# Convolution band in one skewed DRAM write, and w_in in two equal halves around the x load

## Chip, cores and metric

The kernel runs on one core of one Trainium2 chip. The metric is the device time of one execution, in microseconds (us). Before the change the median of 10 runs is 736.57 us (736.01 to 738.22).

## What is computed

A light convolution over the sequence is followed by a two-layer network with an ELU. The input x is (8, 4096, 192), so there are 32768 tokens of 192 channels; weight is (8, 7).

```python
w = softmax(weight, axis=-1)                  # 8 heads, 7 taps
x_pad = 6 zero rows ahead of each sequence
attn[b, s, h*24+g] = sum_k w[h, k] * x_pad[b, s+k, h*24+g]
h = attn.reshape(32768, 192) @ w_in           # (192, 2048)
g = where(h > 0, h, exp(min(h, 0)) - 1)
out = g @ w_out                               # (2048, 192), float32
```

## The kernel before

**Tiling.** The tokens are cut into 32 super-blocks (index s) of 1024, each in two groups of 512. The hidden width 2048 is cut into 16 slices (index q) of 128. One step n is one slice of one super-block, n = 16 s + q. Each step has two units, one per group of tokens. A unit goes through the engines in this order: three w_in matmuls on PE (L794) into a PSUM bank, exp on ACT (L604) into a ring E of 8 buffers, a clamp on GpSimd (POOL, L555), and on DVE the ELU's join (L675), which writes gT and frees the bank. Later the w_out matmuls on PE (L817) read gT, and ACT evacuates their sums (L608) to be stored by SP (L419).

**Convolution.** From the second super-block on, the convolution is a matmul too (L769). Its stationary operand is Tm, [128 x 8 x 112] bf16: for each head a banded matrix in which the seven softmax taps stand on a diagonal. Its moving operand is xg, rows of x in overlapping windows. ACT evacuates it to csb (L600), and a transposing transfer on SP makes att of it (L462). Each super-block has four such steps (m = 4 s + u).

**The first super-block** goes another way, as Tm isn't there yet: x is loaded to xs by ACT's queue (L567), cast by ACT (L583), transposed on PE (L719, L731) and convolved on PE with seven diagonal matrices `taps` (L747), built on DVE (L645).

**How Tm is made.** DVE works out the softmax, in small steps L620 to L631, and their product with the reciprocal goes to wprb, [128 x 8 x 7] bf16 (L654), in reversed tap order; it is the eighth increment of the semaphore s_set. SP then makes the band through DRAM with three transfers. L841 fills conv_band, [128 x 8 x 134], with zeros from the tile zw, once xs has landed. L851 writes the seven taps of each head into row p at an offset that grows by one element per row. L853 reads columns 6 to 117 of each head back into Tm. Each waits for the one ahead of it to land (s_band, 16 each), and L851 also for s_set at 8.

**Orders.** Each engine works through its own list in order. PE's list comes out of a planner (`emit`, `h_items`, `c_items`, `o_items`) with assumed durations; it is fixed at build time. In it the first convolution matmul (m = 4, in step n = 6) waits for s_band at 48 (L759); it also waits for its xg windows (L761). The first w_in matmul of a step waits for that part of w_in which holds its slice q (L785 to L788). The w_out matmuls wait for their half of w_out (L814).

**GpSimd's queue** issues all loads that cast from fp32. At the start it issues, one after the other, w_in's columns 0 to 511 (`load_w_in(0, ...)`, six transfers), columns 512 to 2047 (six more), the first half of w_out (L512), xg for super-block 1 (two transfers, L483), the second half of w_out, and xg for super-block 2. The clamps follow it in its list.

```python
WCOLS = ((0, 4 * FC), (4 * FC, 16 * FC))
load_w_in(0, 0)
load_w_in(0, 1)
load_w_in(1, 0)
load_w_in(1, 1)
load_w_out(0)
for gr in range(2):
    load_x(1, gr)
load_w_out(1)
for gr in range(2):
    load_x(2, gr)
```

Of the kernel before, what the change touches and what calls it, by code (L numbers as in the profile page):

```python
# [8 lines left out]
BF16 = mybir.dt.bfloat16  # L9
# [3 lines left out]
P = 128  # L13
HP = 64
FC = 128
D = 192
HEADS = 8
KSIZE = 7
CPH = 24
CW = 112  # L20
GS = 512
SUP = 2 * GS
PAD = KSIZE - 1
KW = CW + PAD
TW = P + PAD
# [11 lines left out]
QB = 2  # L37
WARM = (15, 1)
FILL = 1
WCOLS = ((0, 4 * FC), (4 * FC, 16 * FC))  # L40
HALO = 8
XI = SUP // P
MM_H, MM_O, MM_C = 216.0, 82.5, 102.5
AHEAD = 100.0
# [11 lines left out]
def bass_lightweight_conv__then__act_elu_kernel(  # L56
# [220 lines left out]
    def tt_count(n, r):  # L277
        return unit_at[n, r] + 1

    band = nc.dram_tensor("conv_band", (P, HEADS, TW), BF16).ap()  # L280

    with ExitStack() as stack:
        def sbuf(name, shape, dt):
            return stack.enter_context(nc.sbuf_tensor(name, shape, dt))
# [4 lines left out]
        def sema(name):  # L289
            return stack.enter_context(nc.semaphore(name))  # L290

        xg = sbuf("xg", [P, NXB, 2 * NWIN, D], BF16)
        Tm = sbuf("Tm", [P, HEADS, CW], BF16)
# [23 lines left out]
        wex = sbuf("wex", [P, HEADS, KSIZE], FP32)  # L317
        wsum = sbuf("wsum", [P, HEADS], FP32)
        wrs = sbuf("wrs", [P, HEADS], FP32)
        wprb = sbuf("wprb", [P, HEADS, KSIZE], BF16)  # L320
        wch = sbuf("wch", [P, KSIZE], FP32)
        zw = sbuf("zw", [P, TW * HEADS], BF16)
        scr = sbuf("scr", [P, 2], FP32)
# [4 lines left out]
        s_set = sema("s_set")  # L328
# [4 lines left out]
        s_xs = sema("s_xs")  # L333
        s_xh = sema("s_xh")
        s_own = sema("s_own")
        s_xz = sema("s_xz")
        s_cast = sema("s_cast")
        s_tap = sema("s_tap")
# [5 lines left out]
        s_zw = sema("s_zw")  # L344
# [7 lines left out]
        s_band = sema("s_band")  # L352
# [114 lines left out]
        @block.gpsimd  # L467
        def _gpsimd(g: bass.BassGpSimd):
            W = Waits(g)

            def load_x(s, gr):
                b = s % NXB
                if s >= NXB:
                    W(s_cv, CU * (s - NXB))
                if s == NXB:
                    W(s_zw, 1)
                def windows(w0, w1, rows):
                    src = bass.AP(
                        tensor=x_flat.tensor,
                        offset=(s * SUP + gr * GS + w0 * CW - PAD) * D,  # L480
                        ap=[[D, rows], [CW * D, w1 - w0], [1, D]],
                    )
                    g.dma_start(  # L483
                        xg[0:rows, b, 2 * w0 + gr : 2 * w1 : 2, :], src
                    ).then_inc(s_x[b][gr], 16)

                if s == NS - 1 and gr == 1:
                    windows(0, NWIN - 1, P)
                    windows(NWIN - 1, NWIN, GS - CW * (NWIN - 1) + PAD)
                else:  # L490
                    windows(0, NWIN, P)

            def batch_zeros(s):

                W(s_x[s % NXB][0], x_need[s, 0])
                g.memset(xg[0:PAD, s % NXB, 0, :], 0.0).then_inc(s_z)

            def load_w_in(k, half):
                c0, c1 = WCOLS[k]
                for j in range(3):  # L500
                    g.dma_start(  # L501
                        w_in[HP * half : HP * (half + 1), j, c0:c1],
                        bass.AP(
                            tensor=moe_w_in.tensor,
                            offset=8 * j * FF + c0,
                            ap=[[CPH * FF, HEADS], [FF, 8], [1, c1 - c0]],
                        ),
                    ).then_inc(s_w[k], 16)

            def load_w_out(k):  # L510
                q = slice(NQ // 2 * k, NQ // 2 * (k + 1))
                g.dma_start(  # L512
                    w_out[:, q, :], moe_w_out.rearrange("(q p) d -> p q d", p=FC)[:, q, :]
                ).then_inc(s_w[2 + k], 16)

            g.memset(ones[:], 1.0).then_inc(s_id)
            W(s_id, 1)
            g.affine_select(
                out=ident[:],
                in_=ones[:],  # L520
                pattern=[[-1, P]],
                compare_op=ALU.is_equal,
                fill=0.0,
                base=0,
                channel_multiplier=1,
            ).then_inc(s_id)
            for step in range(2):
                W(s_id, 2 + step)
                g.affine_select(
                    out=band16[:],  # L530
                    in_=band16[:] if step else ones[:, 0 : 2 * HEADS],
                    pattern=[[8 * (2 * step - 1), 2 * HEADS]],
                    compare_op=ALU.is_ge,
                    fill=0.0,
                    base=7 * step,
                    channel_multiplier=1 - 2 * step,
                ).then_inc(s_id)
            load_w_in(0, 0)
            load_w_in(0, 1)
            load_w_in(1, 0)  # L540
            load_w_in(1, 1)
            load_w_out(0)
            for gr in range(2):
                load_x(1, gr)
            load_w_out(1)
            for gr in range(2):
                load_x(2, gr)
            for i, (n, u) in enumerate(units):
                s, at_n = divmod(i // 2, NQ)
                if i % 2 == 0 and at_n == ZERO_AT and (s + 2) % SPB == 0 and s + 2 < NS:  # L550
                    batch_zeros(s + 2)
                for to_load in x_before.get(i, ()):
                    load_x(*to_load)
                W(s_exp, i + 1)
                g.tensor_scalar(  # L555
                    out=E[:, i % NE, :],
                    in0=E[:, i % NE, :],
                    scalar1=1.0,
                    scalar2=0.0,
                    op0=ALU.min,  # L560
                    op1=ALU.max,
                ).then_inc(s_clp)
# [50 lines left out]
        def _vector(v):  # L613
            W = Waits(v)
            v.memset(zw[:], 0.0).then_inc(s_zw)  # L615
            v.memset(xbh[:, :, 0, :], 0.0).then_inc(s_xz)
            W(s_id, 4)
            v.tensor_tensor(own[:], band16[:, 0:HEADS], band16[:, HEADS : 2 * HEADS], ALU.add).then_inc(s_own)
            W(s_wq, 16)
# [31 lines left out]
            for at, j in enumerate((3, 0)):  # L651
                W(s_xt, at + 1)
                v.tensor_copy(*transposed(j)).then_inc(s_fd)
            v.tensor_tensor(  # L654
                wprb[:, :, ::-1],
                wex[:, 0:HEADS, :],
                wrs[:, 0:HEADS].unsqueeze(2).to_broadcast([P, HEADS, KSIZE]),
                ALU.mult,
            ).then_inc(s_set)
            W(s_first, 2)  # L660
# [3 lines left out]
            for item in dve_order:  # L664
# [4 lines left out]
                i = unit_at[n, u]  # L669
# [15 lines left out]
        def _tensor(pe):  # L685
            W = Waits(pe)
# [15 lines left out]
            for item in pe_order:  # L702
# [52 lines left out]
                elif item[0] == "c":  # L755
                    _, m, rt, q = item
                    s, u = divmod(m, CU)
                    if m == CU:
                        W(s_band, 48)  # L759
                    for gr in range(2):  # L760
                        W(s_x[s % NXB][gr], x_need[s, gr])  # L761
                    W(s_z, z_need[s])
# [4 lines left out]
                    h = HU * u + q  # L767
# [13 lines left out]
                elif item[0] == "h":  # L781
                    _, n, r, j = item
                    s, q = divmod(n, NQ)
                    if j == 0:
                        if q < WCOLS[0][1] // FC:  # L785
                            W(s_w[0], 96)
# [17 lines left out]
                else:  # L804
                    _, k, g, rt, q, kb, visit, ends = item
                    t, half = divmod(k, 2)
# [24 lines left out]
        @block.sync  # L831
        def _sync(sy):
            W = Waits(sy)
            sy.dma_start(
                wq[:, :, :].rearrange("p h k -> p (h k)"),
                bass.AP(tensor=weight.tensor, offset=0, ap=[[0, P], [1, HEADS * KSIZE]]),
            ).then_inc(s_wq, 16)
            sy.dma_start(xh[:, :], x_flat[GS - HALO : GS, :]).then_inc(s_xh, 16)
            W(s_zw, 1)
            W(s_xs, 16)  # L840
            sy.dma_start(  # L841
                band[:, :, :].rearrange("p h t -> p (h t)"), zw[:, :]
            ).then_inc(s_band, 16)
            W(s_band, 16)
            W(s_set, 8)
            diagonal = bass.AP(
                tensor=band.tensor,
                offset=0,
                ap=[[HEADS * TW + 1, P], [TW, HEADS], [1, KSIZE]],
            )  # L850
            sy.dma_start(diagonal, wprb[:, :, :]).then_inc(s_band, 16)  # L851
            W(s_band, 32)
            sy.dma_start(  # L853
                Tm[:, :, :], band[:, :, PAD : PAD + CW]
            ).then_inc(s_band, 16)

            sync_work = []
            for m in range(2 * CU - 1, CU * NS, CU):
                sync_work.append((unit_at_conv[m], ("c", m)))
            sync_work += [(at, item) for at, item in evacs]  # L860
            for _, item in sorted(sync_work):
                if item[0] == "c":
                    transpose(sy, W, item[1] // CU)
                elif item[1:] != (NK - 1, 1):
                    evacuated_by(W, *item[1:])
                    out_group(sy, *item[1:])
            for b in range(2):
                sy.wait_ge(s_out[b], 32 * NS)
# [28 lines left out]
```

## Time and profile before

| what | value |
|---|---|
| median of 10 runs | 736.57 us |
| profiled execution, its own time | 734.79 us |
| its span, first to last instruction | 733.0 us |
| mean granted clock of PE | 0.995 |
| busy, PE / PEld / DVE / ACT / POOL | 98 / 93 / 87 / 92 / 91% |
| chain that ended last: PE / DMA / POOL / ACT | 93 / 4 / 2 / 1% |
| L817 and L794 matmuls in that chain | 52% and 37% of the span |
| landing of w_in's transfers of 64 KB / 192 KB, median after issue | 4.3 / 7.1 us |
| landing of w_out (2) / xg in the first 60 us, longest | 12.9 / 13.7 us |

The engines are PE (matmul), PEld (its weight load), DVE, ACT, POOL (GpSimd) and SP (which only issues transfers here). The chain is followed back from the last instruction to what released each step. A wait is put down to what came last. The "DMA share" of a stretch is the time that packets took, as a share of 16 engines; it exceeds 1 where packets of several queues overlap on an engine. q0 is GpSimd's DMA queue, q1 SP's, q10 ACT's. "Landing" is the time from the issue to the increment of the semaphore.

### The profile page before, as it was taken

How to read it: one execution, taken by the hardware profiler on the slowest of the kernel's cores; microseconds unless marked ns; L12 is line 12 of the kernel's file. 1: busy time of each engine (PE TensorE's matmuls, PEld its weight loads, DVE VectorE, ACT ScalarE, POOL GpSimd, SP SyncE). 2: the span in 40 equal slices, each digit the busy share in tenths (PEclk: the TensorE clock that was granted, in tenths of full speed). 3: DMA queues.
4: the chain of work that ended last, by engine and by line, in shares of the span. 5: the costliest groups of instructions: out<-in, count | busy, mean ns of one | idle time of the engine just before them, and what ended most of it. 6: DMA issues, size and time to landing. Idle time of an engine off the chain costs nothing.

```text
span 733.0 us, 27620 instructions
## 1 busy us (share of the span) xinstructions
PE 721.4 (98%) x11860; PEld 681.2 (93%) x11860; DVE 639.1 (87%) x1041; ACT 677.4 (92%) x1287; POOL 670.5 (91%) x1116
## 2 busy tenths in 40 slices
PE   8699999999999999999999999999999999999998
PEld 4479999999999999999999999999999999999997
DVE  3699999889899889899889898889898889898993
ACT  4699999999999999999999999999999999999993
POOL 7599999999999999999999999999999999999892
PEclk9899999999999999999999999999999999999999
DMA  9626455425355535445534455534445534644212
GB/s 176 82 49 95 72 89 92 79 55 95 72 95 86 69 69 91 73 94 85 89 52 87 77 91 85 86 65 78 81 86 85 95 61 72 92 76 84 69 34 67
DMA packets 134987, 59.20 MB, mean 81 GB/s; under 512 B 101064, under 2 KB 134224, under 8 KB 134864
## 3 DMA queue, kind: packets, MB, share of 16 engines
q1 hardware_dynamic: 90000, 38.87, 23.3%
q0 software_dynamic: 44448, 17.58, 22.7%
q8 instruction: 93, 1.52, 0.8%
q10 hardware_dynamic: 416, 0.98, 0.4%
q14 instruction: 30, 0.25, 0.1%
HBM read 36.20 MB, written 25.45 MB: 84 GB/s over the span
## 4 chain that ended last, share of the span: by engine, by line
PE 93%; DMA 4%; POOL 2%; ACT 1%; DVE 0%; issue 0%; DVEq 0%; SPq 0%
PE H L817 52%; PE H L794 37%; PE H L769 3%; POOL E L555 1%; DMA conv_band<-zw 1%; DMA conv_band<-wprb 1%; ACT E L604 1%; DMA xs<-in_x_dram 1%; DMA Tm<-conv_band 1%; ACT csb L600 0%; POOL xg L483 0%; ACT osb L608 0%; DVE gT L675 0%; DVE osb L666 0%; DVEq L371 0%
## 5 line engine op out<-in xcount | busy, mean ns | idle before, releaser
L675 DVE SCALAR_TENSOR_TENSOR gT<-E,H 128x512 f16<-128x512 f32 x1024 | 633.2, 683 | 72.6 <-POOL E L555 71.2
L817 PE MATMUL H<-w_out,gT 64*128 64x192 f16 x8192 | 684.6, 243 | 0.2
L794 PE MATMUL H<-att,w_in 64*128 64x512 bf16 x3072 | 682.7, 377 | 0.4
L555 POOL TENSOR_SCALAR E<-E 128x512 f32<-128x512 f32 x1024 | 607.2, 612 | 49.3 <-ACT E L604 38.3
L817 PEld LDWEIGHTS H<-w_out,gT 64*128 64x128 f16 x8192 | 626.1, 94 | 22.0 <-PE H L817 2.3
L604 ACT ACTIVATE E<-H 128x512 f32<-128x512 f32 x1024 | 593.6, 601 | 34.9 <-PE H L794 9.3
L794 PEld LDWEIGHTS H<-att,w_in 64*128 64x128 bf16 x3072 | 275.5, 93 | 6.9 <-ACT csb L600 1.3
L769 PE MATMUL H<-xg,Tm 64*112 64x240 bf16 x496 | 93.2, 268 | 6.1 <-DMA Tm<-conv_band 5.8
L600 ACT ACTIVATE csb<-H 112x480 bf16<-112x480 f32 x124 | 70.0, 564 | 0.0
L608 ACT ACTIVATE osb<-H 128x384 f32<-128x384 f32 x127 | 61.7, 486 | 7.5 <-PE H L817 7.4
L769 PEld LDWEIGHTS H<-xg,Tm 64*112 64x112 bf16 x496 | 58.2, 126 | 10.1 <-DMA Tm<-conv_band 6.1
L483 POOL DMA_DIRECT2D xg<-in_x_dram x63 | 56.2, 899 | 0.2 <-issue 0.2
L710 PE MATMUL H<-zw 128*128 128x512 bf16 x21 | 8.3, 530 | 1.5 <-DVE zw L615 1.5
L710 PEld LDWEIGHTS H<-zw 128*128 128x128 bf16 x21 | 2.6, 130 | 6.3 <-issue 4.4
L666 DVE COPY osb<-H 128x384 f32<-128x384 f32 x1 | 0.6, 558 | 8.4 <-PE H L817 8.4
L501 POOL DMA_DIRECT2D w_in<-in_moe_w_in_dram x12 | 6.9, 672 | 0.0
L747 PE MATMUL H<-xT,taps 128*128 128x512 bf16 (+1 forms) x28 | 4.7, 325 | 0.0
L747 PEld LDWEIGHTS H<-xT,taps 128*128 128x128 bf16 x28 | 2.7, 97 | 2.0
L595 ACT ACTIVATE att<-H 128x512 bf16<-128x512 f32 (+1 forms) x2 | 1.0, 490 | 3.7 <-PE H L747 3.7
L620 DVE TENSOR_REDUCE wmx<-wq 128x8 f32<-128x56 f32 x1 | 0.2, 211 | 4.2 <-DMA wq<-in_weight_dram 4.2
L661 DVE CAST att<-H 128x512 bf16<-128x512 f32 x1 | 0.7, 692 | 3.5 <-PE H L747 3.5
L574 ACT ACTIVATE wex<-wq 128x56 f32<-128x56 f32 x1 | 0.2, 250 | 3.8 <-DVE wq L622 3.8
(33 smaller groups left out, 18.4 us busy)
## 6 DMA issues: line engine op xcount, KB each, us to landing
out_dram<-osb SPq DMA_DIRECT2D x127, 192.0 KB, 3.2
xg<-in_x_dram POOLq DMA_DIRECT2D x61, 240.0 KB, 5.0
w_in<-in_moe_w_in_dram POOLq DMA_DIRECT2D x6, 192.0 KB, 7.1
xs<-in_x_dram ACTq DMA_DIRECT2D x1, 768.0 KB, 6.4
w_out<-in_moe_w_out_dram POOLq DMA_DIRECT2D x2, 384.0 KB, 11.8
att<-csb SPq DMA_TRANSPOSE x31, 4.4
w_in<-in_moe_w_in_dram POOLq DMA_DIRECT2D x6, 64.0 KB, 4.3
conv_band<-zw SPq DMA_DIRECT2D x1, 268.0 KB, 8.5
```

The lines of the kernel that those rows point to most:

```text
L483: g.dma_start(xg[0:rows, b, 2 * w0 + gr : 2 * w1 : 2, :], src).then_inc(s_x[b][gr], 16)
L501: g.dma_start(w_in[HP * half : HP * (half + 1), j, c0:c1], bass.AP(tensor=moe_w_in.tensor, offset=8 * j * FF + c0, ap=[[CPH * FF, HEADS], ...
L555: g.tensor_scalar(out=E[:, i % NE, :], in0=E[:, i % NE, :], scalar1=1.0, scalar2=0.0, op0=ALU.min, op1=ALU.max,).then_inc(s_clp)
L600: a.activation(*conv_evac(W, m), ACT.Copy).then_inc(s_ce)
L604: a.activation(E[:, i % NE, :], H[:, bank_of[item], :], ACT.Exp).then_inc(s_exp)
L608: a.activation(*out_evac(W, *item[1:]), ACT.Copy).then_inc(s_oev[item[2]])
L675: v.scalar_tensor_tensor(out=gT[:, s % NG3, q, u, :], in0=E[:, i % NE, :], scalar=1.0, in1=H[:, bank_of[item], :], op0=ALU.subtract, op1=A ...
L710: pe.matmul(H[:, bank, :], zw[:, 0:P], zw[:, 0:GS], start=True, stop=True)
L747: ins = pe.matmul(H[:, bank_of[item] + part, c0:c1], taps[:, tap, :], xT[:, j, HALO - PAD + tap + c0 : HALO - PAD + tap + c1], start=(tap ...
L769: ins = pe.matmul(H[0:CW, bank_of["c", m], 256 * q : 256 * q + UC], Tm[rows, h, :], xg[rows, s % NXB, :, CPH * h : CPH * (h + 1)].rearrang ...
L794: ins = pe.matmul(H[:, bank_of[item[:3]], :], w_in[HP * r : HP * (r + 1), j, FC * q : FC * (q + 1)], att[HP * r : HP * (r + 1), s % 2, j, ...
L817: ins = pe.matmul(acc_of(k, g)[:, D * kb : D * (kb + 1)], gT[HP * rt : HP * (rt + 1), t % NG3, q, g, t0 : t0 + P], w_out[HP * rt : HP * (r ...
```

## The change

The DRAM tensor conv_band becomes a matrix of 128 rows of 8 x 240 + 128 = 2048 elements. A new tile wband, [128 x 8 x 240] bf16, is zeroed by DVE at its start. DVE writes the seven taps of each head into columns 121 to 127 of each head's 240, in place of wprb. SP then writes wband to DRAM in one transfer: row p starts 2049 elements after row p - 1, so that it lies p elements further to the right in its row of 2048. It is read back from column 127 on, 112 columns per head. The first transfer now waits for s_set at 8 and no longer for xs; PE waits for s_band at 32.

In GpSimd's queue the two parts of w_in are both 1024 columns wide, and the second goes behind the first half of w_out and behind xg for super-block 1. Steps with q below 8 wait for the first part, the others for the second.

```diff
-WCOLS = ((0, 4 * FC), (4 * FC, 16 * FC))
+WCOLS = ((0, 8 * FC), (8 * FC, 16 * FC))
+BW = P + CW
...
-    band = nc.dram_tensor("conv_band", (P, HEADS, TW), BF16).ap()
+    band = nc.dram_tensor("conv_band", (P, HEADS * BW + P), BF16).ap()
...
-            load_w_in(1, 0)
-            load_w_in(1, 1)
             load_w_out(0)
             for gr in range(2):
                 load_x(1, gr)
+            load_w_in(1, 0)
+            load_w_in(1, 1)
             load_w_out(1)
...
             v.memset(zw[:], 0.0).then_inc(s_zw)
+            v.memset(wband[:], 0.0).then_inc(s_wb)
             v.memset(xbh[:, :, 0, :], 0.0).then_inc(s_xz)
+            W(s_wb, 1)
             W(s_id, 4)
...
             v.tensor_tensor(
-                wprb[:, :, ::-1],
-                wex[:, 0:HEADS, :],
-                wrs[:, 0:HEADS].unsqueeze(2).to_broadcast([P, HEADS, KSIZE]),
+                wband[:, :, P - KSIZE : P][:, :, ::-1],
+                wex[:, :, :],
+                wrs[:, :].unsqueeze(2).to_broadcast([P, HEADS, KSIZE]),
                 ALU.mult,
             ).then_inc(s_set)
...
                     if m == CU:
-                        W(s_band, 48)
+                        W(s_band, 32)
...
-            W(s_zw, 1)
-            W(s_xs, 16)
+            W(s_set, 8)
             sy.dma_start(
-                band[:, :, :].rearrange("p h t -> p (h t)"), zw[:, :]
+                bass.AP(
+                    tensor=band.tensor,
+                    offset=0,
+                    ap=[[HEADS * BW + P + 1, P], [1, HEADS * BW]],
+                ),
+                wband[:, :, :].rearrange("p h i -> p (h i)"),
             ).then_inc(s_band, 16)
             W(s_band, 16)
-            W(s_set, 8)
-            diagonal = bass.AP(
-                tensor=band.tensor,
-                offset=0,
-                ap=[[HEADS * TW + 1, P], [TW, HEADS], [1, KSIZE]],
-            )
-            sy.dma_start(diagonal, wprb[:, :, :]).then_inc(s_band, 16)
-            W(s_band, 32)
             sy.dma_start(
-                Tm[:, :, :], band[:, :, PAD : PAD + CW]
+                Tm[:, :, :],
+                band[:, P - 1 : P - 1 + HEADS * BW].rearrange("p (h i) -> p h i", h=HEADS)[
+                    :, :, 0:CW
+                ],
             ).then_inc(s_band, 16)
```

More of the change, by code (lines that the diff above doesn't have):

```diff
@@ L319, in bass_lightweight_conv__then__act_elu_kernel @@
         wrs = sbuf("wrs", [P, HEADS], FP32)
-        wprb = sbuf("wprb", [P, HEADS, KSIZE], BF16)
+        wband = sbuf("wband", [P, HEADS, BW], BF16)
         wch = sbuf("wch", [P, KSIZE], FP32)
@@ L335, in bass_lightweight_conv__then__act_elu_kernel @@
         s_own = sema("s_own")
+        s_wb = sema("s_wb")
         s_xz = sema("s_xz")
```

## Prediction

> **What bounds the kernel now.** I read the page's shares first. PE is 98% busy and carries 93% of the chain that ended last, so outside of its gaps the kernel costs what PE's matmuls cost. The next question is whether the change touches matmuls (it doesn't) or a gap. Then I read the chain in order of time: its first pieces are the only long ones of the whole run.
>
> ```profile
> 0.81 6.40 DMA xs<-in_x_dram
> 7.29 8.49 DMA conv_band<-zw
> 15.80 6.99 DMA conv_band<-wprb
> 22.81 4.64 DMA Tm<-conv_band
> 27.49 0.45 PE H L769
> ```
>
> Columns: start, length (us), what. Three transfers stand one after the other, each waiting for the one ahead of it to land, and end at 27.45 us, when the first convolution matmul starts. The waits in the first 60 us say what that costs:
>
> ```profile
> ACT E L604 <- PE H L794: 8.5, 7, 6.4
> PE H L769 <- DMA Tm<-conv_band: 5.8, 1, 5.8
> ...
> SPq L853 <- DMA conv_band<-wprb: 6.6, 1, 6.6
> ...
> SPq L851 <- DMA conv_band<-zw: 5.6, 1, 5.6
> SPq L371 <- DVE wprb L654: 2.5, 1, 2.5
> ```
>
> Columns: total us, times, longest. PE stands 5.8 us for Tm, and behind it ACT (6.4 us), GpSimd (5.7) and DVE (5.4) run empty. PE's order is fixed and the L769 matmul is at the head of its queue, so every later matmul is behind it. Third, the stages around the gap:
>
> ```profile
> 21.00:22.00 1.00, 0.69 (x8) 0.22 (x4) 1.00 (x3) 1.00 (x4) 1.00 (x3) 1.00 2.02 185
> ...
> 23.00:24.00 1.00, 0.00 (x0) 0.00 (x0) 1.00 (x3) 0.00 (x0) 0.88 (x2) 0.91 1.59 190
> 24.00:25.00 1.00, 0.00 (x0) 0.00 (x0) 0.83 (x2) 0.00 (x0) 0.00 (x0) 0.50 1.51 206
> ...
> 27.00:28.00 1.00, 0.51 (x5) 0.46 (x6) 0.00 (x0) 0.00 (x0) 0.00 (x0) 0.50 0.01 2
> ...
> 30.00:32.00 2.00, 1.88 (x20) 1.04 (x18) 1.38 (x2) 1.60 (x4) 1.28 (x3) 0.84 0.00 0
> ```
>
> Columns after the length: PE, PEld, DVE, ACT, POOL busy, granted clock, DMA share, GB/s. PE runs dry at 21.7. Clock 0.91 in 23:24 means that it halved at about 23.8, and 0.84 in 30:32 that it came back at about 30.6: the first 3.1 us after the gap ran at half clock. And the DMA engines are overfull (share over 1) right up to 25 us: the chain's transfers are slow because they share the engines with weights and x.
>
> **The band's three transfers become two.** The zero fill (L841) and the diagonal (L851) become one write of 128 rows of 3840 B, 480 KB, followed by the read (L853), still 1024 runs of 224 B. Start: it now waits for the DVE product at L654, which ended at 9.98 + 0.21 = 10.19. With the issue delays of this trace (0.02 to 0.08) and 0.1 for a later xs (below) the write is issued at 10.4.
>
> How long is the write? Nearest rows by landing: the zero fill, 268 KB in rows of 2144 B, 8.49; the diagonal, 14 KB in 1024 runs, 6.99. Nineteen times the bytes cost 1.5 us more, so bytes are the small part. I looked into both in half-microsecond slices (queue, packets, MB, share of the engines), the zero fill's 11.0:11.5 and 12.5:13.0 first, then the diagonal's 20.0:20.5:
>
> ```profile
> q1 hardware_dynamic: 3, 0.01, 3.8%
> ...
> q0 software_dynamic: 53, 0.07, 71.4%
> q1 hardware_dynamic: 44, 0.09, 48.2%
> ...
> q0 software_dynamic: 236, 0.09, 142.9%
> q1 hardware_dynamic: 236, 0.00, 64.1%
> ```
>
> The zero fill, issued at 7.29, shows no packet before 11.0, then carries data until 15.2: 3.8 us to start and 4 us of data shared with the GpSimd queue (q0), with 0.3 to 0.6 to report. The diagonal likewise starts 3.8 after its issue and carries 2.5 us. The start is the queue in front of it, not size. For 3840-byte rows the 4 us of data has two ends. At the best slice, 0.09 MB in 0.5 us, the extra 217 KB cost 1.2 us; as the zero fill's first and last engine are far apart (11.2 to 15.2), only part of that is added to the slowest one. At worst data time grows with bytes: 4 x 480/268 = 7.2, 3.2 more. Below: a shorter wait as with the diagonal, 7.0 in all. Range 7.0 to 11.7; I take 8.8, close to the zero fill, whose row length, direction and company it shares. It lands at 19.2.
>
> [...]
>
> Read: 4.64 in the row, where its first packets came 1.4 us after issue, with q0 ending as its data moved. In the new program q0 is still busy at 19, so its 3 us of data may stretch: 4.6 to 6.5, I take 5.2. The pitch of its rows becomes 4096 B; no row shows such a pitch, and I give it nothing below and count it in the upper end. Tm lands at 10.4 + 8.8 + 5.2 = 24.4, against 27.45: 3.05 us earlier.
>
> **Does the gain arrive?** PE would run dry at 21.8 as now, and wait 2.6 instead of 5.8. At 24.4 ACT (empty since 22.53) is drained and DVE ends at 24.83, before the first new unit could reach it (2.8 us after the restart in this trace): nothing else holds the restart. From 31 to 47 us ACT is often in the chain, but that stretch has the same work and moves as a block. So the 3.05 goes through.
>
> [...] Our row: halved 2.1 us into the gap, restored 3.15 after its end. [...] The half clock cost: the first ACT unit came 1.44 us after the restart, most of it PE work at half speed, and ACT then idled 0.40 more; some 1 us is to be won. I take none.
>
> **The weight loads.** GpSimd issues the same 18 transfers, 1.84 to 13.97, in another order; only sizes move. First half of w_in: 768 KB instead of 384 ahead of the first L794 matmul. Before, the first 768 KB had been carried by 10.3 (sum of q0's slices), plus about 2 to report: 12.3, needed at 15.15. Hidden; uncovered it would cost its lateness. xg(1) goes from behind 2400 KB (landed near 22.1) to the end of 1632 KB: about 4 us earlier, near 17 to 18, so when Tm is earlier x isn't late instead. The second half of w_in lands where xg(1) did, near 22.5; it is first needed at q=8, some 2 us after the restart, 26. Margin 3.5. w_out(0) moves ahead from 19.3 to about 14; w_out(1) and xg(2) end as before, near 24 and 26.5, and are wanted far later.
>
> xs: from 5.0 to 7.2 it shares engines with w_in, whose rows are now twice as long. Some 56 of its 128 packets, 3 or 4 per engine, alternate with packets of 1024 instead of 512 B, a few tens of ns each: 0.1 later; up to 0.4 if a packet costs its bytes twice over. It delays everything, end included; 0.1 is in the sum.
>
> **Small things.** The new memset, 128x960 words, costs 0.51 x 960/536 = 0.9 us of DVE at 1.5 to 2.4, within its 4.18 us wait for wq (6.28); uncovered it costs 0.9. The product into strided wband stays at 0.21. No instruction is queued on SP behind the two transfers before 36 us. So the sum is Tm's landing alone: -3.05.
>
> **Sum.** Profiled execution: span 733.0, its time 734.79, so 1.8 lies around the span; span after about 730.0. The runs' median, 736.57, is 1.8 above the profiled one; I take the difference to it: 736.57 - 3.05 = 733.5.
>
> **Rivals.** (1) Slower: the write is paid by bytes. 8.49 x 480/268 = 15.2, if the odd row starts (each 4098 B after the last) keep it from sharing well; Tm at 10.4 + 15.2 + 5.2 = 30.8, 3.35 late: 739.9. It decides once the write passes 13.3 us (Tm after 28.9). For it: zero fill is the only large write under load. Against: 3.8 of its 8.49 us passed before any byte. Chance 0.12. (2) No change: write 11 to 12, read 6.5, Tm between 26 and 28.9; the zero fill's data time scaled by bytes leads just there: about 736.6. Chance 0.15. (3) The gap closes: write 7.0, read 4.6, Tm at 22.0, wait 0.2, no half clock; then ACT's 6.4 idle us bound the gain, and DVE, busy to 24.83, holds it nearer 6: 730.6. Chance 0.13. The likeliest, Tm between 23 and 26, gain 1.5 to 4.5, has 0.60.
>
> A measurement of this kernel tells some 0.2%, 1.47 us, from no change. Faster: 0.60 + 0.13 = 0.73; same 0.15; slower 0.12. Range: it leaves out the slower case, and the ends of (2) and (3): 731.0 to 736.8.
>
> **What would show it.** The chain after starts with xs, the write at 10.4, the read near 19, L769 near 24.5. Write landing 7 to 11.7 says right, over 13.3 the first rival. xg or w_in in PE's waits would break the order argument; xs landing after 7.6 the start; clock 1.0 throughout would be the third case.

## The result and the profile after

The changed kernel takes 734.01 us (median of 14 runs, 732.84 to 734.92). Before, measured beside it, it is 736.28 (48 runs). The ratio is 0.9965, 95% interval 0.9959 to 0.9972: a gain of 2.3 us between the medians, 2.1 to 3.0 by the interval, where the prediction had 3.05. The profiled execution took 732.91, its span is 731.0 (733.0 before). Both profiled executions are quick ones: 732.91 is 1.1 below its median, and the 734.79 of before lies below the lowest of the 48 runs (735.09).

The chain in order of time (start, length in us, what), the start of the changed kernel:

```profile
10.28 6.78 DMA conv_band<-wband
17.08 8.28 DMA Tm<-conv_band
25.41 0.45 PE H L773
```

The write was issued at 10.28, as forecast (10.4). It was quicker than any value I had allowed (7.0 to 11.7), and the read slower than any (4.6 to 6.5). The two errors have opposite signs: Tm lands at 25.36 instead of the 24.4 of the sum.

The waits of the first 60 us (total, times, longest) answer to those of before:

```profile
ACT E L606 <- PE H L798: 6.4, 7, 4.2
...
PE H L773 <- DMA Tm<-conv_band: 3.6, 1, 3.6
```

PE's wait fell from 5.8 to 3.6 us and ACT's longest from 6.4 to 4.2. No wait for xg or w_in has come in. The stages around the gap, with the columns as before (the seventh is the granted clock):

```profile
24.00:25.00 1.00, 0.00 (x0) 0.00 (x0) 0.94 (x2) 0.00 (x0) 0.00 (x0) 1.00 1.51 183
25.00:26.00 1.00, 0.59 (x5) 0.54 (x6) 0.00 (x0) 0.00 (x0) 0.00 (x0) 0.64 1.36 161
26.00:27.00 1.00, 1.00 (x12) 0.94 (x8) 0.00 (x0) 0.16 (x1) 0.00 (x0) 0.50 0.57 67
27.00:28.00 1.00, 1.00 (x9) 0.69 (x6) 0.00 (x0) 1.00 (x3) 0.48 (x1) 0.50 0.06 7
28.00:29.00 1.00, 1.00 (x12) 0.72 (x8) 0.69 (x1) 0.54 (x2) 0.67 (x2) 0.65 0.00 0
```

The clock halves only at about 25.3, right when PE gets work again, and is back at about 28.7: the shorter gap still costs a stretch at half clock, 3.4 us long. (In a slice of 1 us at clock c, the part at half clock is 2 x (1 - c): 0.72 of the slice 25:26 and 0.70 of 28:29.) In the kernel before it was 6.8, from 23.82 to 30.64 by the prediction's rows.

Why was the write quick and the read slow? Half-microsecond slices of the queues (queue, packets, MB, share): 14.5:15.0 during the write, then 22.0:22.5 during the read.

```profile
q1 hardware_dynamic: 40, 0.15, 80.7%
q0 software_dynamic: 45, 0.02, 31.3%
...
q0 software_dynamic: 142, 0.05, 86.0%
q1 hardware_dynamic: 143, 0.03, 51.7%
```

In both, SP's queue (q1) and GpSimd's (q0) pass about the same number of packets: 40 to 45, and 143 to 142. In the write one of SP's packets is 3840 B and one of GpSimd's some 0.4 KB (0.02 MB over 45), so SP has 0.15 of the 0.17 MB, and 480 KB are through in 2.1 us but for the last packets (136 of the 144 of SP's queue start between 14.0 and 16.0). In the read SP's packet is 224 B against some 0.4 KB (0.05 MB over 142), and its 1024 packets need 3.7 us but for the last few (1028 of 1040 start between 20.8 and 24.5). My theory, from these counts: the packets of the two queues alternate one for one, so that a transfer beside a full queue is priced by its number of packets, and by whose packets stand between them. 143 against 142 agrees with that. (The counts are sums over all 16 engines, and equal counts don't tell turns of single packets of the profile from turns of equal groups of them, so "one for one" here means equal numbers in half a microsecond.) Rivals: the order of the loads did the work; the bytes decide; the read's 4096-byte pitch slows it.

### The profile page after: what moved, and what is told of

It is laid out like the page before. It is cut to its first block, busy times and chain, and to the rows that moved or that the text cites. A ratio compares the mean times of both kernels' runs of the same rounds, so it can differ in the third digit from the quotient of the medians.

```text
span 731.0 us, 27620 instructions
## 1 busy us (share of the span) xinstructions
PE 720.5 (99%) x11860; PEld 680.8 (93%) x11860; DVE 639.8 (88%) x1042; ACT 677.2 (93%) x1287; POOL 670.4 (92%) x1116
## 3 DMA queue, kind: packets, MB, share of 16 engines
q0 software_dynamic: 44448, 17.58, 22.8%
## 4 chain that ended last, share of the span: by engine, by line
PE 93%; DMA 3%; POOL 2%; ACT 1%; DVE 1%; issue 0%; DVEq 0%
PE H L821 53%; PE H L798 37%; PE H L773 3%; POOL E L557 1%; DMA Tm<-conv_band 1%; DMA conv_band<-wband 1%; ACT E L606 1%; DMA wq<-in_weight_dram 1%; ACT csb L602 0%; POOL xg L485 0%; DVE taps L649 0%; ACT osb L610 0%; DVE gT L679 0%; DVE xT L657 0%; DVE osb L670 0%
## 5 line engine op out<-in xcount | busy, mean ns | idle before, releaser
L821 PEld LDWEIGHTS H<-w_out,gT 64*128 64x128 f16 x8192 | 626.3, 94 | 21.8 <-PE H L821 2.4
```

The lines of the kernel that those rows point to most:

```text
L821: ins = pe.matmul(acc_of(k, g)[:, D * kb : D * (kb + 1)], gT[HP * rt : HP * (rt + 1), t % NG3, q, g, t0 : t0 + P], w_out[HP * rt : HP * (r ...
```

## The experiments

**Each part alone.** The band alone keeps the old `WCOLS` and the old order of the loads; the loads alone keep the old band.

```diff
-            load_w_in(1, 0)     # loads alone: only these, and WCOLS, as in the change
-            load_w_in(1, 1)
             load_w_out(0)
             for gr in range(2):
                 load_x(1, gr)
+            load_w_in(1, 0)
+            load_w_in(1, 1)
```

> The changed band, with the loads in the order and sizes of before. My theory (packets of SP's queue and GpSimd's alternate one for one on each engine, and each SP transfer first waits some 3.7 us when that queue is full): the write is issued at 10.3 and meets w_in's longer packets, so it takes 8 to 10 us instead of 6.8; the read starts near 19, meets w_out and x and takes 7 to 8; Tm lands at 26 to 27, PE waits 4 to 5 us, time about 735.5, a gain of 0.5 to 1.5 on before. If instead the order of the loads plays no part in Tm's chain, the gain is the whole 2.3 us: 734.0. x for super-block 1 lands near 22 in both and is not waited for.

Measured: 734.09 us, ratio 0.9970 (0.9959 to 0.9982). The write took 7.66, the read 8.07, and PE started on Tm at 26.05, 0.6 later than with both parts. Tm's landing, 26.0, is as expected, though the write was a little quicker than its 8 to 10. The time isn't: it is that of the expectation's second case, and cannot be told from that of the whole change. So the order of the loads adds nothing that can be measured to the new band. In this profile PE came to the wait later (22.2 instead of 21.8), and the clock halved only at 27.1.

> The new order and halves of the loads, with the band of before in three transfers. My theory: the zero fill (issued near 7.4) meets w_out's short packets and lands in 7 to 8 us, the diagonal in 7, and the read starts near 22 beside x and w_out that now end near 26 to 27, so it takes 6 to 8 instead of 4.6: Tm at 28 to 29.5, time 736.5 to 738, no gain or a loss of 1. If the order itself were what helped (x earlier), it would show a gain of 1 to 2 us with the three transfers still there.

Measured: 734.61 us, ratio 0.9977 (0.9970 to 0.9984): a gain of 1.6, where I had expected none. The zero fill, now beside short packets, took 5.76 instead of 8.49, the diagonal, now beside w_in's, 9.22 instead of 6.99 (I had expected 7), and the read 4.63, with Tm at 27.05. Against the first profile of before that is 0.4 us, not 1.6. The expectation's mechanism was right for the zero fill, and wrong for the read: its first packet came 1.6 us after its issue, just as GpSimd's queue ran out. Where the rest of the 1.6 is, two more profiles of before's chain (below) go some way to tell.

**The read in long runs.** Each row's 3584 B in one run, which moves twice the bytes in an eighth of the packets:

```diff
-        Tm = sbuf("Tm", [P, HEADS, CW], BF16)
+        Tm = sbuf("Tm", [P, HEADS, BW], BF16)
...
+            row = (HEADS - 1) * BW + CW
...
-                Tm[:, :, :],
-                band[:, P - 1 : P - 1 + HEADS * BW].rearrange("p (h i) -> p h i", h=HEADS)[
-                    :, :, 0:CW
-                ],
+                Tm[:, :, :].rearrange("p h i -> p (h i)")[:, 0:row], band[:, P - 1 : P - 1 + row]
...
-                        Tm[rows, h, :],
+                        Tm[rows, h, 0:CW],
```

> The changed kernel, but the read fetches each row's 3584 bytes in one run (128 runs in all, into a wider Tm whose unused columns lie between the heads) instead of 1024 runs of 224 bytes. It moves twice the bytes. My theory (one packet of SP's queue for one of GpSimd's): 8 long packets per engine instead of 64 short ones, data in about 2 us as the write had instead of 3.7, start unchanged near 3.6 us: landing 6 to 6.5 instead of 8.3, Tm near 23.3, time 732. Rival (the read is slow by DRAM load or by its 4096-byte pitch): twice the bytes at the same pitch, landing 8.3 or more, time 734 or more.

Measured: 729.96 us, ratio 0.9914 (0.9900 to 0.9927). The read landed in 6.2 us. The slice 21.0:21.5 of this kernel:

```profile
q1 hardware_dynamic: 43, 0.15, 82.2%
q0 software_dynamic: 47, 0.02, 37.0%
```

Again about as many packets of the one as of the other, but SP's 43 now carry 0.15 MB, where the short read's 143 carried 0.03. Twice the bytes took 2.1 us less: bytes as the price, and the pitch (still 4096), fall. The time fell by 4.1 us, 2 more than expected: the clock stayed at 1.00 throughout, which by the test below is worth about 1.7. PE started at 23.54 after a wait of 1.4.

**Less beside the read.** The second half of w_out and x for super-block 2 are issued behind the first 12 clamps (`if i == 12:` in GpSimd's loop).

> The changed kernel, with the second half of w_out and x for super-block 2 issued by GpSimd behind its first 12 clamps, when PE, ACT and GpSimd stand, instead of ahead of them. GpSimd's queue then ends with the second half of w_in near 19.5 to 20.5. My theory: the write is as before it (6.8), the read (issued at 17.1) has the engines for itself from about 20 on, so its data takes 2.5 us instead of 3.7 and its start is 2 to 3.5: landing 5 to 6.5, Tm 22 to 23.5, PE's wait 0.5 to 2, time 731 to 732.5. Rival (pitch): read still 8.3, time 734. What can spoil it: x for super-block 2 or w_out's second half late at step 12 to 14, seen as a wait of PE for xg or w_out.

Measured: 731.30 us, ratio 0.9938 (0.9925 to 0.9950). The read took 5.9; its first packets came 1.9 us after the issue, as GpSimd's queue thinned out. PE started at 23.06 with no halved clock. It is no better than the long read, because the three issues themselves now stand between clamps: they hold GpSimd from 24.15 to 26.8, and DVE waits for it. That cost I had not put in.

**Half clock.** 14 matmuls on zeros ahead of the wait, into the bank that the convolution then overwrites:

```diff
+                    if m == CU and rt == 0 and q == 0:    # once, ahead of the first
+                        wait_bank(("c", m))
+                        for _ in range(GAP):    # 14
+                            pe.matmul(
+                                H[:, bank_of["c", m], :], zw[:, 0:P], zw[:, 0:GS], start=True, stop=True
+                            )
                     if m == CU:
                         W(s_band, 32)
```

> The changed kernel, with 14 matmuls on zeros put into PE's queue just ahead of the wait for Tm (into the bank that the convolution then overwrites), so that PE isn't idle in the gap. Tm lands as before it, near 25.4. If the half clock after the gap (25.4 to 28.6 in the changed kernel) is paid in time, the clock stays at 1.0 and the time falls by 1 to 2 us, to 732 to 733. If ACT sets the pace after the restart anyway, as the prediction's low end for it had it, nothing moves: 734.0. Loss only if the 14 matmuls (3.0 us) outlast the wait (3.6 us).

Measured: 732.30 us, ratio 0.9944 (0.9931 to 0.9956), clock 1.00 throughout, with Tm at 25.5. So in the changed kernel some 1.7 us of the time were the half clock's, with the same landing. The chain shows that the zeros took a little back:

```profile
22.64 3.19 PE H L766 x14
25.83 0.24 PE H L780
```

Columns: start, length (us), what. L766 is the matmul on zeros, L780 the convolution: PE was free for Tm 0.3 us after its landing.

**The write in short runs.** The access pattern of the write becomes [[2049, 128], [240, 8], [1, 239]].

> The changed kernel, with the write cut into 1024 runs of 478 bytes (239 of each head's 240 columns; the last is never read), so the same bytes in short packets. My theory (packets alternate one for one with GpSimd's queue): 64 packets per engine, data 3.7 to 4.2 us instead of 2.1, landing 8.3 to 9.3 instead of 6.8, the read then near 8, Tm at 26.5 to 27.5, time 735 to 736. Rival (bytes decide): landing 6.8, time 734.0.

Measured: 739.34 us, ratio 1.0043 (1.0029 to 1.0056): 3 us slower than before, and over 3 slower than I had expected. The write took 12.29 us for the same bytes that took 6.78, so packets, not bytes. But it is worse than one pair per packet at the read's pace. Slice 16.5:17.0:

```profile
q0 software_dynamic: 80, 0.07, 82.3%
q1 hardware_dynamic: 76, 0.04, 29.7%
```

The numbers are still nearly equal (76 to 80), but a pair takes 105 ns of an engine (16 x 500 ns / 76), where the read's pairs took 56 (16 x 500 / 143). The shares tell whose packets grew: by them one of q0's, now w_in's rows among them, took 82 ns (82.3% of 16 x 500 / 80) where it had taken 48 beside the read, and one of SP's 31 against 29. So the short writes were hardly slower in themselves than the short reads; the neighbour's longer packets stood between them. The two times of a pair overlap in part, so they don't add up to it.

**The pitch.** Rows 4272 B apart instead of 4096 (the row step of the write grows by the same 88 elements):

```diff
-    band = nc.dram_tensor("conv_band", (P, HEADS * BW + P), BF16).ap()
+    band = nc.dram_tensor("conv_band", (P, HEADS * BW + P + 88), BF16).ap()
```

> The changed kernel, with the DRAM rows 4272 instead of 4096 bytes apart on reading (4274 instead of 4098 on writing). My theory: the pitch plays no part, write 6.8, read 8.3, time 734.0. Rival (the read is slow because its rows lie a power of two apart): read 4.6 to 7, Tm 22 to 24, time 730 to 733.

Measured: 733.72 us, ratio 0.9960 (0.9948 to 0.9973); write 6.27, read 8.94. The read isn't helped by this other pitch, and the long read was quick at 4096; that rival falls. This profile also shows a part of the time that is chance: PE's gap is that of the changed kernel (21.76 to 25.48, against 21.80 to 25.41), but the clock halved 1.0 us sooner, at 24.31, and stayed so for 6.8 us instead of 3.4; its execution took 733.93, 1.0 more.

**Narrow rows.** 128 columns per head (`BW = P`), rows of 1136 elements written and 1008 read, each in one run.

> The long read and narrower rows: 128 columns per head instead of 240, which is the least that keeps one head's taps out of the next one's window. The write is 128 rows of 2272 bytes, the read 128 runs of 2016. My theory: packets per engine as in the long read, each shorter; starts stay at 3.6, data of both 1.3 to 1.8 us, write 6.2 to 6.7, read 5.3 to 5.9 (6.2 with 3584 bytes), Tm at 21.9 to 22.9, PE's wait under 1 us, time 729 to 729.9, 0 to 1 below the long read. If bytes decided instead, the write would fall to 4 and the read to 3.5, Tm before 19.

Measured: 729.38 us, ratio 0.9904 (0.9891 to 0.9918), the lowest median of all, within the interval of the long read's. Write 6.35 and read 6.12, with PE on Tm at 22.86. The bytes of the write fell from 480 to 284 KB and its landing only from 6.78 to 6.35, no more than the same write differs from profile to profile (6.2 to 7.3 in five kernels with the changed kernel's band and loads ahead of it).

**The write earlier.** On top of that, DVE's product into wband stands right behind the reciprocal, and SP waits for s_set at 5.

> The narrower rows and the long read, with DVE's product into wband moved up to right behind the reciprocal, ahead of wown, wsel, wch, taps and the two xT copies. The write is issued at 7.7 instead of 10.3; start 3.6, so that it meets w_in's and w_out's packets: landing 6 to 7, read from 14.2, landing 5.5 to 6.5, Tm at 19.5 to 21, ahead of PE's arrival at 21.8: no wait for Tm. The product's 0.21 us now lies ahead of taps on the way to the first matmul, so that everything starts 0.2 later. Against 729.4 with the product late: 0.95 us of waiting saved, 0.2 paid, 728.6. If ACT and DVE, still busy with the units ahead, hold the restart, 729.2. Rival: x for super-block 1 takes the wait's place, seen as PE waiting for xg.

Measured: 729.44 us, ratio 0.9904 (0.9889 to 0.9920): no gain. The write went out at 7.91 and Tm landed at 20.3, well ahead of PE. Yet PE's first matmul on it, as the timeline shows it (start, length; in brackets the idle time and its releaser):

```profile
22.80 0.28 PE L774 MATMUL H<-xg,Tm 64*112 64x240 bf16 x1 [0.90 <-DVE gT L680]
```

PE now waits 0.9 us for DVE to free a PSUM bank (the next run, where Tm is early too, has the same start, 22.82). So 22.8 is the floor under Tm's landing, and of the 3.6 us that PE waits in the changed kernel only 2.6 (25.41 - 22.8) were Tm's to give.

**The read into empty engines.** All of w_in's second half also goes behind the first 12 clamps.

> The changed kernel, with the second half of w_in also issued behind the first 12 clamps, so that GpSimd's queue is empty from about 16 to 24. The write is unchanged (6.8, as it meets the short packets of w_out and x). The read is issued at 17.1 into an empty set of engines. If the 3.6 us to its first packet are the full queue's doing: first packet after 1.4 to 2.0, data 2.4, landing 4.0 to 4.7, Tm at 21.1 to 21.8 and no wait for it. If 3.6 us belong to such a transfer anyway: landing 6 or more. The kernel as a whole gets slower, since the second half of w_in then lands near 31 and step 8 needs it near 25: 736 to 740.

Measured: 738.21 us, ratio 1.0019 (1.0012 to 1.0027). PE waits 7.2 us for w_in, the loss that the expectation names, and the whole is a little slower than before. But the read by itself took 3.2 us, issued at 16.53 with its first packets near 17.6, and in its slice 18.0:18.5 there is one queue:

```profile
q1 hardware_dynamic: 550, 0.12, 116.2%
```

550 packets where 143 passed beside GpSimd's queue. (The share passes 100% with one queue alone, so packets of the same queue overlap on an engine too.) Of the read's 8.28 us, 5.1 belong to the company it kept: some 2.5 to its first packet, the rest to its data.

**The kernel before once more, and without half clock.**

> The kernel before, unchanged, for a second profile. The first profiled execution (734.79) lies below the lowest of the 48 times of that kernel (735.09), so its chain may be shorter than the usual one. If so, Tm lands later than 27.45 here, by up to 1.5 us, and the loads' order alone (734.6, a gain of 1.6 with a profile that shows only 0.4 us of it) is explained by that. If Tm lands at 27.4 again, the spread lies after the restart, in how long the clock stays halved: 3.1 us in the first profile, 4.8 with the loads alone.

Measured: 737.00 us, ratio 0.9999 (0.9989 to 1.0009). This profiled execution took 737.45, and its chain is another:

```profile
7.00 7.29 DMA conv_band<-zw
14.30 7.68 DMA conv_band<-wprb
22.00 7.43 DMA Tm<-conv_band
```

Tm lands at 29.43, 2 us later than in the first profile. And w_out's first half landed 12.7 us after its issue instead of 10.8, which held PE's first w_out matmul:

```profile
21.36 0.24 PE L817 MATMUL H<-w_out,gT 64*128 64x192 f16 x1 [1.94 <-DVE gT L675]
```

(The releaser named had long been done; w_out landed at 21.2. With zero matmuls, below, the profile names w_out for a wait of 0.97 at the same place.) So ahead of the 5.8 us for Tm lay another wait with no margin at all: in the first profile w_out landed at 19.3 and was used at 19.4. The new order of the loads takes it away. It counts only where Tm isn't later anyway: here Tm came 8 us later and PE would have stood for it all the same, so this wait explains none of what the loads alone gain in the profiles at hand.

The half clock of this profile, its first and its last slice:

```profile
27.00:28.00 1.00, 0.00 (x0) 0.00 (x0) 0.00 (x0) 0.00 (x0) 0.00 (x0) 0.92 0.21 32
34.00:35.00 1.00, 1.00 (x12) 0.88 (x10) 0.69 (x1) 0.45 (x1) 0.67 (x2) 0.67 0.00 0
```

It lasted from 27.84 to 34.66, 6.8 us as in the first profile.

> The kernel before, with 23 matmuls on zeros (4.9 us) in PE's queue ahead of the wait for Tm. Tm as before it. The changed kernel won 1.7 us from such matmuls; if the half clock after the gap costs the same here, 734.5, and the change's gain with PE kept busy in both is 734.5 - 732.3 = 2.2, all of it Tm's landing. If the kernel before loses more to the clock than the changed one, it gains over 2.2 here, and a part of the change's gain was the clock's.

Measured: 735.04 us, ratio 0.9982 (0.9971 to 0.9994): 1.4 us, against 1.7 in the changed kernel, which the intervals do not tell apart. With PE kept busy in both, the change is worth 0.9982 - 0.9944 = 0.0038, 2.8 us (1.5 to 4 by the two intervals), with no half clock in it. ACT's first unit after the gap starts at 29.68 here and at 26.60 in the changed kernel with such matmuls, 3.1 apart: what the change gains is Tm's landing, and the clock's part is the same in both as far as the intervals go.

Tm landed at 28.80 here. With 27.45 and 29.43, the three profiles of before's chain have a mean of 28.6; the loads alone (27.05) are 1.5 ahead of it, about their gain of 1.6. That is a fit over single profiles, no proof. The changed kernel's 25.36 is 3.2 ahead.

The granted clock of each run shows what the profiles can't. Six of the 14 runs of the changed kernel have 0.997 or 0.998, with a median of 733.28 us; the other eight have 0.994 or 0.995, and 734.18. None of the 74 runs of the kernel before that stood beside the experiments is above 0.995. So by the clock six of the changed kernel's runs have the shorter stretch of 3.4 us, as its profile does (0.998), and eight one of 6.8, as the profile of the pitch (0.995); the kernel before has the longer one at least. The two groups are 0.9 us apart.

## Why the prediction was right, and where its steps failed

- **Where the gain lies.** Right. One wait, for Tm, and nothing in the steady part; the chain after it moves as a block. The third ACT evacuation of the convolution after the restart starts 2.04 us earlier (33.91 to 31.87), the span ends 2.0 earlier.
- **The start of the write**: right, 10.28 against 10.4. xs landed 6.5 us after its issue instead of 6.4, the 0.1 of the estimate; but over all profiles it is 6.5 to 6.9 with the new loads (ten) and 5.3 to 6.4 with the old (four), so the term was rather too small.
- **"The write takes 8.8, close to the zero fill, whose row length, direction and company it shares".** This step failed; it took 6.78. The row length wasn't shared (3840 B against 2144), nor was the company: the new order puts w_out's and x's short packets beside the write, and the term "4 us of data" was 2.1. With the old loads beside it (the band alone) it took 7.66, so the order may have made up to 0.9 of the 2.0 that I was off, though the same write also took 6.2 to 7.3 with the new loads. The rest is the size of the term: a row is one packet in both, of 162 ns in the median in the write (128 of 3840 B) and 100 in the first profile's zero fill (128 of 2144 B), and two other profiles of before's chain have the zero fill at 7.29 and 7.46, so that my 8.49 was a long one.
- **"Read 5.2, with 3 us of data that may stretch".** This step failed more: 8.28. I took the 1.4 us to the first packet from a read that was issued as GpSimd's queue was running out. Beside a full queue it was 3.7, nearly the 3.8 that I had seen for both writes and had put into the write's sum only. The data took 3.7. The row itself was a short draw: in the two other profiles of before's chain this read took 7.43 and 6.43, not 4.64.
- **The sum.** Tm 1 us later than forecast: -2.0 from the write, +3.1 from the read, -0.1 from the start. The gain of 3.05 became 2.1 between the first two profiles and 2.3 between the medians. The likeliest case, 1.5 to 4.5, held; that both wrong terms nearly cancelled was luck. So was the base: Tm at 27.45 is the earliest of three, and against a later one a Tm at 24.4 would have promised more.
- **The clock.** Taking no gain for it was right to within what can be measured: halved in both, and 1.4 and 1.7 us to be won by zeros. "Some 1 us is to be won" was too little by about half. What it left out is that after the same gap the half clock lasted 3.4 us in the changed kernel's profile and 6.8 in that of the other pitch, and that by the clock six of the changed kernel's 14 runs have the shorter one.
- **The slower rival** (write paid by bytes, 15.2) is refuted by the write at 6.78, and by 284 and 480 KB landing 0.4 us apart. The rival that the gap closes came true only in other kernels: its 730.6 stands against 729.4 with Tm at 22.8, a gain of 7 rather than 6, and as it said, DVE holds the restart from there.
- **What I missed**: w_out's zero margin in the kernel before, hidden behind Tm's wait, and that one profile may show a chain 2 us shorter than another of the same kernel.

Open: why a transfer on SP's queue sees its first packet 3.5 to 4.2 us after its issue while GpSimd's queue is full, whatever the length of the packets there (1.5 to 2.7 when that queue was near its end, 1.1 when it was empty; but also 1.9 for the read of the short-write kernel, with q0 still at 139% in that half microsecond); and how the 1.6 us of the loads alone divide between Tm's landing and the clock, as that kernel has one profile only.

## What to carry to other kernels

Where two queues share the DMA engines, price a transfer by its packets and its neighbour's: one long run per row, even with bytes that nobody uses, beat eight short ones here (8.3 to 6.2 us with twice the bytes). Each transfer that waited for another to land paid anew before its first packet, 3.5 to 4.2 us here beside GpSimd's queue at full load (in one read only 1.9), 1.1 with that queue empty. Take a duration only from a row that kept the same company, look at what the neighbouring queue does in that very stretch, and take a second profile: the same read took 4.6, 6.4 and 7.4 us in three. A gap of PE cost its length and then the half clock behind it: here 1.7 us after a wait of 3.6 and 1.4 after one of 5.8, which matmuls on zeros won back; after waits of 0.8 to 1.9 the clock stayed at 1.00.

## What the runs showed of the hardware

Beside a full queue, SP's packets and GpSimd's came out nearly equal in number in the half microseconds shown (143 to 142 in the short read, 43 to 47 in the long one, 76 to 80 in the short write). In the read of the short-write kernel they did not: 95 to 215 in 25.0:25.5. The same read took 3.2 us with the engines empty and 8.3 beside a full queue. A write of 478 KB took 12.3 us in 1024 runs, and one of 480 KB 6.8 in 128, and while the short runs passed (14.5 to 19.5), GpSimd's queue was slowed too, from 0.10 MB in half a microsecond ahead of them to 0.06 to 0.08.

PE's clock halved 2.1 us after PE fell idle in one profile of before, 4.2 in the other (dry at 23.6, halved at 27.84 by its 0.92 in 27:28), 3.5 in the changed kernel, and 4.9 with the band alone, when PE had been at work again for 1 us; it stayed at 1.00 through waits of 0.8 to 1.9 us. It stayed halved for 3.4 us in the changed kernel and with the band alone, 6.8 in both profiles of before, with the loads alone, with the other pitch and with w_in deferred, and 10.2 with the short writes (24.2 to 34.4): in these profiles, once, twice and three times 3.4.
